# An operand made earlier, denser weight conversions and a shared mixing step in an attention and channel-mix kernel

## The chip, the cores and the metric

The kernel runs on one core of a Trainium2 chip. The metric is the device time in microseconds (us), the median of several runs. Beside the runs there is one profiled execution, from which the page and all answers of the trace come.

## The reference

```python
def _attn_ref(q, k, v):                      # q, k, v: 8 x 12 x 448 x 64
    scale = 1.0 / np.sqrt(q.shape[-1])
    scores = scale * np.matmul(q, k.transpose(0, 1, 3, 2)) - np.log(S)
    attn = 1.0 / (1.0 + np.exp(-scores))
    return np.matmul(attn, v).astype(np.float32)

def _moe_ref(x, mu_k, mu_r, w_k, w_v, w_r):  # x: 8 x 448 x 768, heads side by side
    x_prev = np.concatenate([np.zeros((B, 1, D)), x[:, :-1, :]], axis=1)
    xk = mu_k * x + (1.0 - mu_k) * x_prev
    xr = mu_r * x + (1.0 - mu_r) * x_prev
    k = np.maximum(xk @ w_k, 0.0)            # w_k: 768 x 1024
    v = k * k @ w_v                          # w_v: 1024 x 768
    r = 1.0 / (1.0 + np.exp(-(xr @ w_r)))    # w_r: 768 x 768, the "receptance"
    return (r * v).astype(np.float32)
```

The attention uses a sigmoid of each score and no sum over a row. Its output, with heads side by side, is the input of the channel mix. Inputs are scaled in `setup_inputs`. The weights arrive as 64-bit floats.

## The kernel before, in words

**Attention (lines 447 to 473).** 48 pairs of heads are taken two at a time, so 24 rounds ("pairs" from here on, since the code's index `n` steps by two), each of NV = 7 steps over blocks of 64 keys. In a step TensorE computes scores into `sc` (line 317), ScalarE turns them into probabilities `pf` (one sigmoid of 128 x 896 elements, line 320), and two steps later (`LAG`) TensorE multiplies them with the values into `av` (line 329). `sc` has two buffers in PSUM, `pf` has `PFB` = 4 in SBUF, `raw` (queries and keys) and `vn` (values) have six each, so their loads are issued two rounds before they are needed. `av` has four PSUM banks, two per round.

After the seventh step of a round `gather` (lines 336 to 346) mixes each finished head pair with its own copy shifted by one position. It does so twice, for `xr` and for `xk`: GpSimd sets the first column to zero, VectorE multiplies the shifted rows by 1 − mu (line 344), VectorE adds mu times the rows (line 345), and SP stores the result `xo` to HBM as `xr_d` or `xk_d`. `xo` has eight buffers.

**Conversions (lines 204 to 277).** VectorE turns each 64-bit weight into float32 by bit operations (lines 211 to 216), reading `wraw` (two buffers) and writing one of the seven `wbit` buffers; line 244 then forms sums and differences. Each call of `convert_next` does one block. During attention there are 24 blocks: twelve of `w_r`, whose results are split into two parts in the `slot` tiles (lines 289 and 290), and twelve of `w_k`, whose results are stored to HBM as `wk_o`. The 16 blocks of `w_v` come in the second plan and are stored as `wv_o`.

**Mixing half (lines 477 to 597).** Three stages: receptance (`xr` times `w_r`), key (`xk` times `w_k`), value (squared keys times `w_v`). Each goes over four pairs of token groups (`s` = 0 to 3; a group is one batch of 448 tokens). For such a pair a matrix product in two by two blocks is done with seven products instead of eight, in `ORDER` = (0, 1, 4, 5, 6, 2, 3). Every product needs one operand from the tokens: `right` fetches rows into a y buffer (`fetch`, line 394; SP), subtracts others where needed (`minus`, line 402; VectorE), and `operand` splits the result into a high part (a cast on ScalarE, line 408) and a remainder (VectorE, line 409). A matmul in float32r runs three times, high by high, high by remainder and remainder by high (line 524), into PSUM banks `xb` or `yb`. `evacuate` combines banks and writes results (lines 537 to 576), and `load_weight` brings the next stage's weights into the slots (lines 508 to 510) during the last pass of a stage.

The operand's home comes from `take`: a ring of four in stages 0 and 1, two in `rra` and two in `rrb`, and three larger ones in stage 2. The y buffers come from `y_of`: roles 0 and 1 in `ysa`, 2 and 3 in `ysb`. `rra` and `ysa` lie in a pool that exists from the start; `rrb` and `ysb` lie in the pool `kp`, opened where attention's buffers (`raw`, `vn`, `pf`, `xo`) lay, so each of its tiles has to wait for the old tiles at its place.

**The order of the work.** Both halves are planned by `Plan`: each operation has an engine, a modelled cost, a priority (the argument `at`) and dependencies, and a list scheduler picks on each engine the ready operation with the lowest priority number. Its result fixes the order on each engine; every engine then runs its queue in order. The two plans are emitted one after the other, each in a block of manual order; operations of the second may slip between those of the first on an engine. The planner does not know dependencies between reads of the same data.

Before the change the operands of products 0 and 1 of the first pair are planned in the attention half:

```python
    right(0, 0, 0, N - 6)
    right(0, 0, 1, N - 5)
```

and product 4, the third, is the first of the second plan that needs `ysb` and `rrb`.

Of the kernel before, what the change touches and what calls it, by code (L numbers as in the profile page):

```python
# [22 lines left out]
class Plan:  # L23
# [7 lines left out]
    def op(self, engine, cost, prio, run, reads, writes, dma=None):  # L31
        i = len(self.ops)
        deps = set()
        for r in reads:
            if r in self.writer:
                deps.add(self.writer[r])
        for w in writes:
            if w in self.writer:
                deps.add(self.writer[w])
            deps.update(self.readers.get(w, ()))  # L40
        for r in reads:
            self.readers.setdefault(r, []).append(i)
        for w in writes:
            self.writer[w] = i
            self.readers[w] = []
        deps.discard(i)
        self.ops.append(Op(engine, cost, prio, run, deps, dma))
# [51 lines left out]
def attention_then_channel_mix(  # L99
# [15 lines left out]
    nc = tc.nc  # L115
# [36 lines left out]
    wk_o = [dram.tile([P, WO], F32, name=f"wk_o{p}") for p in range(7)]  # L152
    wv_o = [dram.tile([P, WO], F32, name=f"wv_o{p}") for p in range(7)]

    WP, PFB, RAW, WB = 512, 4, 6, 7

    def ring(pool, name, bufs, shape, dtype):
        return [pool.tile(shape, dtype, name=f"{name}{i}") for i in range(bufs)]
# [3 lines left out]
    slots = [wp.tile([P, 2 * WO], F32R, name=f"slot{g}") for g in range(7)]  # L162
    RU = 2 * NJH
    wp.tile([P, 16], F32, name="gap0")
    rra = wp.tile([P, 2 * RU, TB], F32R, name="rra")
    ysa = wp.tile([P, RU, TB], F32, name="ysa")
    wraw = wp.tile([P, 2, WP, 2], U32, name="wraw")
    wbit = wp.tile([P, WB, WP], U32, name="wbit")
# [19 lines left out]
    def act(n, sbuf=False, ptr=False):  # L188
        return 51 + 0.834 * n + 42 * sbuf + 93 * ptr

    def dve(n, fast=False, ptr=False):
        return 69 + n / (1.92 if fast else 0.96) + 61 * ptr
# [143 lines left out]
    def gather(n, at):  # L336
        b, j = divmod(n, NP)
        x, X = av[bank(n)], ("av", bank(n))
        for mu, om, dst, key in ((mur, omr, xr_d, "xr_d"), (muk, omk, xk_d, "xk_d")):
            u = nxo[0] % len(xo)  # L340
            nxo[0] += 1
            y, Y = xo[u], ("xo", u)
            op(POOL, 200, at, lambda y=y: nc.gpsimd.memset(y[:, 0:1], 0.0), [], [Y])
            op(DVE, dve(S, ptr=True), at, lambda y=y, om=om: nc.vector.tensor_scalar_mul(y[:, 1:], x[:, :S - 1], om[:, j:j + 1]), [X, ("om", key)], [Y])  # L344
            op(DVE, dve(S, ptr=True), at, lambda y=y, mu=mu: nc.vector.scalar_tensor_tensor(y, x[:, :S], mu[:, j:j + 1], y, ALU.mult, ALU.add), [X, Y], [Y])  # L345
            dma(dst[b][:, j], y, at, [Y], [(key, n)])

# [5 lines left out]
    def units(name, u, n):  # L353
        return big[name][:, u:u + n], [("wraw", x % 2) if name == "wraw" else (name, x) for x in range(u, u + n)]

    def y_of(stage, role):
        if stage < 2:
            return units(("ysa", "ysb")[role // 2], role % 2 * NJH, NJH)
        return units(("wbit", "ysb", "ysa", "wraw")[role], 0, NFH)

    first_of_value = 2 * NS * 7

    def take(stage):
        u = rr_n[0]
        rr_n[0] += 1
        if stage < 2:
            name, at = ("rra", "rrb")[u % 4 // 2], u % 2 * RU
            return units(name, at, NJH), units(name, at + NJH, NJH)
        u -= first_of_value
        if u % 3 < 2:  # L370
            name = ("rra", "rrb")[u % 3]
            return units(name, 0, NFH), units(name, NFH, NFH)
        return units("rra", 2 * NFH, NFH), units("rrb", 2 * NFH, NFH)

    def pieces(g):
        lo, hi, found = g * TB, (g + 1) * TB, []
# [2 lines left out]
            found.append((b, slice(x0 - b * S, x1 - b * S), slice(x0 - lo, x1 - lo)))  # L379
        return found  # L380

    def fetch(stage, g, ch, role, at):
        y, Y = y_of(stage, role)
        n = TILES[stage]
        rows = slice(ch * n, (ch + 1) * n)
        if stage == 2:
            dma(y, k2_d[g][:, rows], at - 0.5, [("k2_d", g, f) for f in range(ch * n, (ch + 1) * n)], Y)
            return
        src, key = ((xr_d, "xr_d"), (xk_d, "xk_d"))[stage]
        parts = pieces(g)  # L390

        def go():
            for b, cs, cd in parts:
                nc.sync.dma_start(y[:, :, cd], src[b][:, rows, cs])

        reads = [(key, b * NP + j) for b, _, _ in parts for j in range(ch * n, (ch + 1) * n)]
        op(SP, 500 * len(parts), at - 0.5, go, reads, Y, dma=P * n * TB * 4 / 300)

    def minus(stage, dst, a, b, at):
        (d, D_), (x, X), (y, Y) = (y_of(stage, r) for r in (dst, a, b))  # L400
        for t in range(TILES[stage]):
            op(DVE, dve(TB), at, lambda t=t: nc.vector.tensor_sub(d[:, t], x[:, t], y[:, t]), [X[t], Y[t]], [D_[t]])  # L402

    def operand(stage, role, keys, at):
        y, Y = y_of(stage, role)
        (hi, H), (lo, L) = take(stage)
        for t in range(TILES[stage]):
            op(ACT, act(TB, True), at, lambda t=t: nc.scalar.copy(hi[:, t], y[:, t]), [Y[t]], [H[t]])  # L408
            op(DVE, dve(TB), at, lambda t=t: nc.vector.tensor_sub(lo[:, t], y[:, t], hi[:, t]), [Y[t], H[t]], [L[t]])  # L409
        for k in keys:  # L410
            used[k] = (hi, lo, H + L)

    def right(stage, s, p, at):
        g0, g1 = 2 * s, 2 * s + 1
        key = [(stage, s, p)]
        if p == 0:
            fetch(stage, g0, 0, 0, at)
            operand(stage, 0, key, at)
        elif p == 1:
            fetch(stage, g0, 1, 1, at)  # L420
            operand(stage, 1, key, at)
        elif p == 4:
            fetch(stage, g1, 0, 2, at)
            minus(stage, 0, 2, 0, at)
            operand(stage, 0, key, at)
        elif p == 5:
            fetch(stage, g1, 1, 3, at)
            minus(stage, 0, 3, 0, at)
            operand(stage, 0, key, at)
            minus(stage, 1, 1, 0, at)  # L430
        elif p == 6:
            minus(stage, 2, 3, 2, at)
            operand(stage, 2, key, at)
        elif p == 2:
            operand(stage, 3, key, at)
        else:
            operand(stage, 1, key, at)

    for n in range(4):
        load(n, -9 + n // 2 * 2)  # L440
# [6 lines left out]
    def convert_next(at, after):  # L447
        try:
            work.send((at, after))
        except StopIteration:  # L450
            pass
# [3 lines left out]
    for t in range(T + LAG):  # L455
        n, j = t // NV * 2, t % NV
        if t < T:
            if j == 0:
                convert_next(n + 8, n - 2 if n else None)
            score(n, j, t, n + j / NV)  # L460
        if t < LAG:
            continue
        n, j = (t - LAG) // NV * 2, (t - LAG) % NV
        weigh(n, j, t - LAG, n + j / NV)
        if j == NV - 1:
            for m in (n, n + 1):
                gather(m, m)
                if m + 4 < N:
                    load(m + 4, n + 0.5)
    right(0, 0, 0, N - 6)  # L470
    right(0, 0, 1, N - 5)
    with tc.manual_schedule():
        plan.emit()
    att.close()
    ps.close()

    kp = ctx.enter_context(tc.tile_pool(name="kp", bufs=1, side="right", reuse_waits="tile"))
    rrb = kp.tile([P, 2 * RU, TB], F32R, name="rrb")
    ysb = kp.tile([P, RU, TB], F32, name="ysb")
    big["rrb"], big["ysb"] = rrb, ysb  # L480
    p1s = ring(kp, "p1s", 4, [P, TB], F32)
# [30 lines left out]
    def multiply(stage, s, p, i, at):  # L512
        xs = p in (0, 1, 4, 2)
        bank, K = (xb[i], ("xb", i)) if xs else (yb[i], ("yb", i))
        first = p in (0, 5, 4)
        hi, lo, R = used[stage, s, p]
        whi, wlo, W = slot_of(stage, p)
        n, w = TILES[stage], WIDTH[stage]

        def go():  # L520
            for t in range(n):
                c = slice(t * w + i * P, t * w + (i + 1) * P)
                for e, (a, b) in enumerate(((whi[:, c], hi[:, t]), (whi[:, c], lo[:, t]), (wlo[:, c], hi[:, t]))):
                    nc.tensor.matmul(bank, a, b, start=first and t == 0 and e == 0, stop=t == n - 1 and e == 2, skip_group_check=True)  # L524

        reads = R + [W + (h, a) for h in range(WO // WC) for a in ("hi", "lo")]
        op(PE, mm(3 * n, TB), at, go, reads, [K])
# [50 lines left out]

    work = conversions(((2, w_v, put_dram(wv_o, WIDTH[2])),))
    next(work)  # L580
    for a in range(4 * TILES[2]):
        convert_next(2 + 2.5 * a, None)
    PREP, EVAC = -1.0, 0.3
    at = 0
    for stage in range(3):
        for s in range(NS):
            for p in ORDER:
                if (stage, s, p) not in used:
                    right(stage, s, p, at + PREP)
                for i in range(ROWS[stage]):  # L590
                    multiply(stage, s, p, i, at + i / ROWS[stage])
                    evacuate(stage, s, p, i, at + i / ROWS[stage] + EVAC)
                if stage < 2 and s == NS - 1:
                    load_weight(stage + 1, p, at + 1.2)
                at += 1
# [36 lines left out]
```

## Time and profile before

| what | value |
|---|---|
| median of 3 runs | 829.41 us (829.18 to 830.04) |
| profiled execution, its own time | 828.44 us |
| profiled execution, span from first to last instruction | 826.7 us |
| TensorE matmuls, busy | 811.3 us, 98% of the span |
| VectorE busy | 643.5 us, 78% |
| ScalarE busy | 444.7 us, 54% |
| DMA, mean rate over the span | 217 GB/s |
| mean granted TensorE clock | 0.995 |

The profiled execution's own time holds the span and 1.7 us around it. In the profile a row of a group names line, engine, operation, output and inputs by the program's tile names, the shapes and the count; behind the bar stand the busy time and the mean duration of one in ns; behind the second bar stands the engine's idle time just before these instructions and what ended most of it. PE is TensorE, DVE VectorE, ACT ScalarE, POOL GpSimd, SP SyncE, which issues all DMAs here. Rows of a timeline have the start, the duration up to the last one's end, and the count of merged instructions. Attention takes the span from 3.6 to 258.2 us, the mixing half the rest.

### The profile page before, as it was taken

Reading aid. Unit: us, or ns where it says so; the run is one execution under the profiler, and the core shown is the slowest. Engines: PE = TensorE matmul, PEld = TensorE weight load, DVE = VectorE, ACT = ScalarE, POOL = GpSimd, SP = SyncE. Lnnn points to the kernel's source line nnn. Section 1 sums busy time; section 2 is a strip of 40 time slices with the busy share of each in tenths; the row PEclk is TensorE's granted clock in tenths of the full one; section 3 lists DMA queues with packets and bytes.
Section 4 is the critical chain, followed back from the end, with each engine's and each line's share of the span. In section 5 each row is a group of like instructions: output and inputs, shape, how many; then the busy total and the mean of one; then the engine's idle time right before and its main releaser. Section 6 shows DMA issues by size and latency. Waiting matters only on the chain.

```text
span 826.7 us, 15158 instructions
## 1 busy us (share of the span) xinstructions
PE 811.3 (98%) x5460; PEld 638.0 (77%) x5460; DVE 643.5 (78%) x1200; ACT 444.7 (54%) x743; POOL 9.7 (1%) x100
## 2 busy tenths in 40 slices
PE   8999999999999699999999999999999999999997
PEld 3444444444446599999999999999999999999997
DVE  1988787878786799999999738466697794977955
ACT  5777666666663444546684746647694333333320
POOL 0000000000000000000000000000000000000000
PEclk9999999999999899999999999999999999999999
DMA  8897778898974777585969542422765546755414
GB/s 283 283 314 260 247 253 267 295 326 299 330 239 153 264 254 249 162 274 171 349 219 309 199 148 90 157 93 108 267 219 187 173 145 198 223 179 177 136 45 156
DMA packets 94203, 179.80 MB, mean 217 GB/s; under 512 B 10544, under 2 KB 74544, under 8 KB 94128
## 3 DMA queue, kind: packets, MB, share of 16 engines
q1 hardware_dynamic: 94128, 178.83, 64.9%
q8 instruction: 43, 0.70, 0.4%
q14 instruction: 32, 0.26, 0.1%
HBM read 109.06 MB, written 69.73 MB: 216 GB/s over the span
## 4 chain that ended last, share of the span: by engine, by line
PE 96%; DVE 2%; DMA 1%; issue 1%; ACT 0%; SPq 0%; DVEq 0%; ACTq 0%
PE xb L524 37%; PE yb L524 29%; PE sc L317 15%; PE av L329 15%; DMA ysb<-xr_d 1%; DVE xo L345 0%; DMA raw<-in_qk 0%; DVE xo L344 0%; DVE wbit L215 0%; DVE wbit L214 0%; DVE wbit L216 0%; DVE wbit L244 0%; DVE ysa L402 0%; DVE cc L576 0%; DVE cc L549 0%
## 5 line engine op out<-in xcount | busy, mean ns | idle before, releaser
L320 ACT ACTIVATE pf<-sc 128x896 f32<-128x896 f32 x168 | 154.0, 917 | 90.4 <-PE sc L317 90.2
L524 PE MATMUL xb<-rra,slot 128*128 128x448 f32 x828 | 180.7, 362 | 0.0
L524 PE MATMUL xb<-rrb,slot 128*128 128x448 f32 x756 | 167.4, 365 | 7.1 <-ACT cc L537 7.1
L317 PE MATMUL sc<-raw 64*64 64x448 f32 x1344 | 161.6, 541 | 3.6 <-DMA raw<-in_qk 3.6
L524 PEld LDWEIGHTS xb<-rra,slot 128*128 128x128 f32 x828 | 155.2, 188 | 10.9 <-issue 0.7
L329 PE MATMUL av<-pf,vn 64*64 64x448 f32 x1344 | 159.7, 536 | 0.0
L524 PEld LDWEIGHTS xb<-rrb,slot 128*128 128x128 f32 x756 | 142.8, 189 | 17.6 <-ACT cc L537 7.5
L524 PE MATMUL yb<-rra,slot 128*128 128x448 f32 x630 | 134.6, 362 | 0.0
L524 PEld LDWEIGHTS yb<-rra,slot 128*128 128x128 f32 x630 | 118.1, 188 | 7.8
L524 PE MATMUL yb<-rrb,slot 128*128 128x448 f32 x558 | 119.7, 362 | 0.0
L317 PEld LDWEIGHTS sc<-raw 64*64 64x64 f32 x1344 | 58.8, 134 | 72.4 <-issue 63.4
L329 PEld LDWEIGHTS av<-pf,vn 64*64 64x64 f32 x1344 | 58.4, 133 | 67.9 <-issue 66.8
L524 PEld LDWEIGHTS yb<-rrb,slot 128*128 128x128 f32 x558 | 104.7, 188 | 7.0
L408 ACT CAST rrb<-ysa 128x448 fp32r<-128x448 f32 x68 | 36.9, 562 | 39.6 <-DVE ysa L402 13.3
L344 DVE TENSOR_SCALAR xo<-av,omr 128x447 f32<-128x447 f32 x48 | 32.5, 677 | 31.9 <-PE av L329 31.6
L408 ACT CAST rra<-ysa 128x448 fp32r<-128x448 f32 x68 | 36.9, 561 | 27.1 <-PE xb L524 10.5
L562 DVE TENSOR_TENSOR u<-yb,p1s 128x448 f32<-128x448 f32 x40 | 24.9, 621 | 30.0 <-PE yb L524 29.8
L409 DVE TENSOR_TENSOR rra<-ysa,rra 128x448 fp32r<-128x448 f32 x64 | 37.5, 616 | 7.7 <-ACT rra L408 7.7
L560 ACT COPY p1s<-xb 128x448 f32<-128x448 f32 x40 | 21.1, 529 | 39.1 <-PE xb L524 39.0
L409 DVE TENSOR_TENSOR rrb<-ysa,rrb 128x448 fp32r<-128x448 f32 x68 | 39.6, 616 | 0.2 <-ACT rrb L408 0.2
L542 ACT ACTIVATE cc<-cc 128x448 f32<-128x448 f32 x48 | 27.5, 577 | 19.4 <-DVE cc L568 13.2
L408 ACT CAST rra<-ysb 128x448 fp32r<-128x448 f32 x44 | 23.9, 565 | 26.0 <-PE yb L524 14.3
(57 smaller groups left out, 744.2 us busy)
## 6 DMA issues: line engine op xcount, KB each, us to landing
k_d<-cc SPq DMA_DIRECT2D x64, 224.0 KB, 2.1
raw<-in_qk SPq DMA_DIRECT2D x48, 256.0 KB, 4.1
vn<-in_v SPq DMA_DIRECT2D x48, 224.0 KB, 5.2
xr_d<-xo SPq DMA_DIRECT2D x48, 224.0 KB, 3.8
xk_d<-xo SPq DMA_DIRECT2D x48, 224.0 KB, 3.8
r_d<-cc SPq DMA_DIRECT2D x48, 224.0 KB, 2.7
out<-cc SPq DMA_DIRECT2D x48, 224.0 KB, 3.0
raw<-in_qk SPq DMA_DIRECT2D x48, 192.0 KB, 4.2
```

The source lines that it names most:

```text
L317: nc.tensor.matmul(u[half[h ^ (m % 2)], m % 2, :S], x[half[h], c], x[half[h], D:D + S], start=True, stop=True)
L320: op(ACT, act(2 * S), at, lambda: nc.scalar.activation(f, u[:, :, :S], AF.Sigmoid, bias=NEG_LOG_S, scale=SCALE), [("sc", t % 2)], [("pf", ...
L329: nc.tensor.matmul(av[bank(m)][half[r ^ (m % 2)], :S], vn[m % RAW][half[r], j, :], pf[t % PFB][half[r], m % 2, :], start=j == 0, stop=j == ...
L344: op(DVE, dve(S, ptr=True), at, lambda y=y, om=om: nc.vector.tensor_scalar_mul(y[:, 1:], x[:, :S - 1], om[:, j:j + 1]), [X, ("om", key)], [Y])
L408: op(ACT, act(TB, True), at, lambda t=t: nc.scalar.copy(hi[:, t], y[:, t]), [Y[t]], [H[t]])
L409: op(DVE, dve(TB), at, lambda t=t: nc.vector.tensor_sub(lo[:, t], y[:, t], hi[:, t]), [Y[t], H[t]], [L[t]])
L524: nc.tensor.matmul(bank, a, b, start=first and t == 0 and e == 0, stop=t == n - 1 and e == 2, skip_group_check=True)
L542: op(ACT, act(TB), at, lambda: nc.scalar.activation(c, src, AF.Relu), R, [C])
L560: op(ACT, act(TB), at, lambda: nc.scalar.copy(p1s[i], x), [X], [P1])
L562: op(DVE, dve(TB), at, lambda: add(u2[i], y, p1s[i]), [Y, P1], [U2])
```

## The change

- The operand of product 4 of the first pair of receptance is made within the attention half, like those of products 0 and 1. For it `rra` grows from two to three places of operands and `rrb` shrinks from two to one, and `y_of` puts roles 2 and 3 of the very first pair into `wbit` instead of `ysb`. `PFB` goes from 4 to 3.
- `take` goes round the same four places (and three larger ones in the last stage), now counted through `rra` and on into `rrb`.
- The 24 conversions of the attention half are spread over 18 rounds instead of 24: in every third round two are called. Their priority is `n + 4` instead of `n + 8`.
- The 16 conversions of `w_v` begin at the eighth product of the mixing half and come at every second product, instead of at 2, 4.5, 7 and so on.
- In `gather` the multiplication of the shifted rows for `xk` is done by ScalarE (`nc.scalar.mul` with a per-partition factor); that for `xr` stays on VectorE, and so do both additions.

```diff
-    WP, PFB, RAW, WB = 512, 4, 6, 7
+    WP, PFB, RAW, WB = 512, 3, 6, 7
...
-    rra = wp.tile([P, 2 * RU, TB], F32R, name="rra")
+    rra = wp.tile([P, 3 * RU, TB], F32R, name="rra")
...
-            op(DVE, dve(S, ptr=True), at, lambda y=y, om=om: nc.vector.tensor_scalar_mul(y[:, 1:], x[:, :S - 1], om[:, j:j + 1]), [X, ("om", key)], [Y])
+            if key == "xr_d":
+                op(DVE, dve(S, ptr=True), at, lambda y=y, om=om: nc.vector.tensor_scalar_mul(y[:, 1:], x[:, :S - 1], om[:, j:j + 1]), [X, ("om", key)], [Y])
+            else:
+                op(ACT, act(S, ptr=True), at, lambda y=y, om=om: nc.scalar.mul(y[:, 1:], x[:, :S - 1], om[:, j:j + 1]), [X, ("om", key)], [Y])
...
-    def y_of(stage, role):
+    def y_of(stage, s, role):
+        if stage == s == 0 and role > 1:
+            return units("wbit", (role - 2) * NJH, NJH)
         if stage < 2:
             return units(("ysa", "ysb")[role // 2], role % 2 * NJH, NJH)
...
     def take(stage):
         u = rr_n[0]
         rr_n[0] += 1
+        n = TILES[stage]
         if stage < 2:
-            name, at = ("rra", "rrb")[u % 4 // 2], u % 2 * RU
-            return units(name, at, NJH), units(name, at + NJH, NJH)
-        u -= first_of_value
-        if u % 3 < 2:
-            name = ("rra", "rrb")[u % 3]
-            return units(name, 0, NFH), units(name, NFH, NFH)
-        return units("rra", 2 * NFH, NFH), units("rrb", 2 * NFH, NFH)
+            at = [u % 4 * RU + t for t in range(RU)]
+        else:
+            at = [(u - 2 * NS * 7) % 3 * 2 * n + t for t in range(2 * n)]
+        found = []
+        for x in at:
+            name, x = ("rra", x) if x < 3 * RU else ("rrb", x - 3 * RU)
+            found.append((big[name][:, x], (name, x)))
+        return tuple(zip(*found[:n])), tuple(zip(*found[n:]))
...
             if j == 0:
-                convert_next(n + 8, n - 2 if n else None)
+                for _ in range(1 + (n % 6 == 4)):
+                    convert_next(n + 4, n - 2 if n else None)
...
-    right(0, 0, 0, N - 6)
-    right(0, 0, 1, N - 5)
+    for p in ORDER[:3]:
+        right(0, 0, p, N - 6 + p)
...
-    rrb = kp.tile([P, 2 * RU, TB], F32R, name="rrb")
+    rrb = kp.tile([P, RU, TB], F32R, name="rrb")
...
-    for a in range(4 * TILES[2]):
-        convert_next(2 + 2.5 * a, None)
...
                 if (stage, s, p) not in used:
                     right(stage, s, p, at + PREP)
+                if at >= 7 and at % 2 == 0:
+                    convert_next(at + 1, None)
```

`fetch`, `minus`, `operand` and `right` take the pair's index `s` as a further argument and pass it to `y_of`, and the high and remainder parts of an operand are now tuples of single tiles (`hi[t]` in place of `hi[:, t]`).

More of the change, by code (lines that the diff above doesn't have):

```diff
@@ L359, in y_of @@
         return units(("wbit", "ysb", "ysa", "wraw")[role], 0, NFH)
-    first_of_value = 2 * NS * 7
     def take(stage):
@@ L380, in pieces, with fetch @@
         return found
-    def fetch(stage, g, ch, role, at):
-        y, Y = y_of(stage, role)
+    def fetch(stage, s, g, ch, role, at):
+        y, Y = y_of(stage, s, role)
         n = TILES[stage]
@@ L397, in fetch, with minus, operand @@
         op(SP, 500 * len(parts), at - 0.5, go, reads, Y, dma=P * n * TB * 4 / 300)
-    def minus(stage, dst, a, b, at):
-        (d, D_), (x, X), (y, Y) = (y_of(stage, r) for r in (dst, a, b))
+    def minus(stage, s, dst, a, b, at):
+        (d, D_), (x, X), (y, Y) = (y_of(stage, s, r) for r in (dst, a, b))
         for t in range(TILES[stage]):
             op(DVE, dve(TB), at, lambda t=t: nc.vector.tensor_sub(d[:, t], x[:, t], y[:, t]), [X[t], Y[t]], [D_[t]])
-    def operand(stage, role, keys, at):
-        y, Y = y_of(stage, role)
+    def operand(stage, s, role, keys, at):
+        y, Y = y_of(stage, s, role)
         (hi, H), (lo, L) = take(stage)
         for t in range(TILES[stage]):
-            op(ACT, act(TB, True), at, lambda t=t: nc.scalar.copy(hi[:, t], y[:, t]), [Y[t]], [H[t]])
-            op(DVE, dve(TB), at, lambda t=t: nc.vector.tensor_sub(lo[:, t], y[:, t], hi[:, t]), [Y[t], H[t]], [L[t]])
+            op(ACT, act(TB, True), at, lambda t=t: nc.scalar.copy(hi[t], y[:, t]), [Y[t]], [H[t]])
+            op(DVE, dve(TB), at, lambda t=t: nc.vector.tensor_sub(lo[t], y[:, t], hi[t]), [Y[t], H[t]], [L[t]])
         for k in keys:
-            used[k] = (hi, lo, H + L)
+            used[k] = (hi, lo, list(H + L))
     def right(stage, s, p, at):
@@ L416, in right @@
         if p == 0:
-            fetch(stage, g0, 0, 0, at)
-            operand(stage, 0, key, at)
+            fetch(stage, s, g0, 0, 0, at)
+            operand(stage, s, 0, key, at)
         elif p == 1:
-            fetch(stage, g0, 1, 1, at)
-            operand(stage, 1, key, at)
+            fetch(stage, s, g0, 1, 1, at)
+            operand(stage, s, 1, key, at)
         elif p == 4:
-            fetch(stage, g1, 0, 2, at)
-            minus(stage, 0, 2, 0, at)
-            operand(stage, 0, key, at)
+            fetch(stage, s, g1, 0, 2, at)
+            minus(stage, s, 0, 2, 0, at)
+            operand(stage, s, 0, key, at)
         elif p == 5:
[L427 to L430, printed above, removed]
+            fetch(stage, s, g1, 1, 3, at)
+            minus(stage, s, 0, 3, 0, at)
+            operand(stage, s, 0, key, at)
+            minus(stage, s, 1, 1, 0, at)
         elif p == 6:
-            minus(stage, 2, 3, 2, at)
-            operand(stage, 2, key, at)
+            minus(stage, s, 2, 3, 2, at)
+            operand(stage, s, 2, key, at)
         elif p == 2:
-            operand(stage, 3, key, at)
+            operand(stage, s, 3, key, at)
         else:
-            operand(stage, 1, key, at)
+            operand(stage, s, 1, key, at)
     for n in range(4):
@@ L522, in go @@
                 c = slice(t * w + i * P, t * w + (i + 1) * P)
-                for e, (a, b) in enumerate(((whi[:, c], hi[:, t]), (whi[:, c], lo[:, t]), (wlo[:, c], hi[:, t]))):
+                for e, (a, b) in enumerate(((whi[:, c], hi[t]), (whi[:, c], lo[t]), (wlo[:, c], hi[t]))):
                     nc.tensor.matmul(bank, a, b, start=first and t == 0 and e == 0, stop=t == n - 1 and e == 2, skip_group_check=True)
```

## The prediction

> **What bounds the kernel now.** I read the page's head and its matmul groups first, then TensorE's waits, then the chain around the one stall, then each engine's timeline there.
>
> ```profile
> PE 811.3 (98%) x5460; PEld 638.0 (77%) x5460; DVE 643.5 (78%) x1200; ACT 444.7 (54%) x743; POOL 9.7 (1%) x100
> L524 PE MATMUL xb<-rra,slot 128*128 128x448 f32 x828 | 180.7, 362 | 0.0
> L524 PE MATMUL xb<-rrb,slot 128*128 128x448 f32 x756 | 167.4, 365 | 7.1 <-ACT cc L537 7.1
> L524 PE MATMUL yb<-rra,slot 128*128 128x448 f32 x630 | 134.6, 362 | 0.0
> L524 PE MATMUL yb<-rrb,slot 128*128 128x448 f32 x558 | 119.7, 362 | 0.0
> ...
> PE xb L524 <- ACT cc L537: 7.1, 1, 7.1
> PE sc L317 <- DMA raw<-in_qk: 3.6, 1, 3.6
> ```
>
> TensorE is the bound at 98%, and it waits only twice: at the start for its first load, and once for 7.1 us in the mixing half. The chain shows where, the clock windows what it costs beyond that.
>
> ```profile
> 269.96 4.71 DMA ysb<-xr_d
> 274.69 0.64 DVE ysa L402
> 275.82 0.55 ACT cc L537
> 276.41 7.29 PE xb L524 x27
> 305.31 16.20 PE xb L524 x81
> 814.72 7.22 PE yb L524 x36
> ...
> 258.22 11.08 PE L524 MATMUL xb<-rra,slot 128*128 128x448 f32 x54
> 276.41 7.29 PE L524 MATMUL xb<-rrb,slot 128*128 128x448 f32 x27 [7.10 <-ACT cc L537]
> ...
> 272.50:276.40 3.90, 0.00 (x0) 0.00 (x0) 1.71 (x4) 1.05 (x3) 0.00 (x0) 0.55 0.97 384
> 276.40:279.70 3.30, 3.29 (x8) 2.78 (x9) 3.30 (x7) 2.45 (x6) 0.00 (x0) 0.50 1.06 397
> ```
>
> In steady state 81 matmuls take 16.20 us, 0.200 each. Products 0 and 1 (54 matmuls, 10.80 us) run from 258.22; the third, product 4, should follow at 269.02 and starts at 276.41: 7.39 us lost. Its 27 matmuls then take 7.29 instead of 5.40, 1.89 us more, and the granted clock says why: 0.50 until 279.7. Together 9.28. Check: the four groups hold 2772 matmuls, 554.4 us at 0.200, and the chain runs from 258.22 to 814.72 + 7.22 = 821.94, which is 563.72: 9.3 us over, so the rest of the mixing half has no stall. That is the pool to win.
>
> Why product 4 is late:
>
> ```profile
> 246.21 0.33 SPq L202 DMA_DIRECT2D wraw<-in_moe_w_v  x1
> 269.55 0.32 SPq L202 DMA_DIRECT2D xk_d<-xo  x1
> 269.96 0.90 SPq L394 DMA_DIRECT2D ysb<-xr_d  x2
> ...
> 254.32 0.36 DVE L212 TENSOR_SCALAR wbit<-wraw 128x384 uint32<-128x384 uint32 x1 [6.08 <-DMA wk_o<-wbit]
> 254.59 0.68 DVE L344 TENSOR_SCALAR xo<-av,omr 128x447 f32<-128x447 f32 x1
> 258.14 0.68 DVE L345 SCALAR_TENSOR_TENSOR xo<-av,mur,xo 128x448 f32<-128x448 f32 x1
> 258.73 0.68 DVE L345 SCALAR_TENSOR_TENSOR xo<-av,muk,xo 128x448 f32<-128x448 f32 x1
> 259.32 0.42 DVE L212 TENSOR_SCALAR wbit<-wraw 128x512 uint32<-128x512 uint32 x1
> 262.78 0.35 DVE L213 TENSOR_SCALAR wexpo<-wraw 128x384 uint32<-128x384 uint32 x1
> 268.84 0.68 DVE L345 SCALAR_TENSOR_TENSOR xo<-av,muk,xo 128x448 f32<-128x448 f32 x1
> ```
>
> Its fetch stands on SP behind the last mixed rows (269.55), and these are late on VectorE: a conversion sat 6.08 us waiting for a buffer's store, the gather of the last pair but one came after it, another conversion followed (259.32 to 262.78), and the last gather ended at 269.5, though attention ended at 258.2.
>
> **The change part by part.**
>
> *Third operand in attention.* One fetch, three subtractions, three casts and three remainders move from after 269.96 to inside attention; the fetch needs batch 1, stored early, and weight buffers that the earlier conversions leave free. On SP it is one issue of about 0.4 us, ahead of loads that stand two pairs (21 us) before their use. On VectorE six operations by the 0.53 us of the start-to-start steps (three take 1.70), 3.2 us, on ScalarE three casts: beside TensorE, whose steps cover them, so zero on the path; uncovered they would cost at most what they cost today, the 6.45 us from 269.96 to 276.41. After attention TensorE then has 3 × 5.40 = 16.2 us of products instead of 10.8, to 274.4. The fourth operand (product 5) is late next: its fetch now writes weight buffers, so it waits for nothing that attention's end releases, and SP issues such a thing early when it can (the `in_moe_w_v` load at 246.21 belongs to the second plan). Gain: 7.39, and with no idle time no half clock: 1.89.
>
> The Trainium skill (TensorE: Matmul & The Clock Gate, Part 1) says that the array's clock falls to half after an idle window of about 3.4 us and rises after as much activity; the trace agrees, with 0.50 to 0.55 after 272.5. By that rule an idle rest shorter than the window costs only itself.
>
> *Conversions in fewer cycles.* 24 conversions move from 24 pairs into 18 (four per three pairs). One costs VectorE 3.46 us (259.32 to 262.78); per pair of 10.5 us that adds 1.15, while the mixing gives 2 × 0.59 = 1.19 to ScalarE. VectorE stays at its mean, and for the last six pairs it has only the gather. So neither the 6.08 us wait nor the conversion at 259.32 stands before the last gather, which should end near 263, not 269.5. DMA is the other side:
>
> ```profile
> 214.40:224.90 10.50, 10.50 (x116) 4.87 (x112) 9.21 (x17) 6.40 (x8) 0.42 (x5) 1.00 1.00 351
> 4.00:256.50 252.50, 252.50 (x2672) 116.43 (x2672) 190.88 (x348) 163.45 (x195) 9.14 (x88) 1.00 0.83 280
> ...
> wraw<-in_moe_w_k SPq DMA_DIRECT2D x12, 512.0 KB, 6.4
> wk_o<-wbit SPq DMA_DIRECT2D x21, 256.0 KB, 4.5
> ```
>
> A third of a conversion more per pair in the second nine pairs is (512 + 21/12 × 256)/3 = 320 KB, some 31 GB/s. The busiest pair of now, the row with 351, ran at a full share without a PE stall; a backlog of a few us meets a lead of 21. I take zero; bounds 0 and the waits priced in the third rival.
>
> *Mixing on ScalarE.* 48 multiplications, two per pair, in front of the sigmoids in ScalarE's queue:
>
> ```profile
> L560 ACT COPY p1s<-xb 128x448 f32<-128x448 f32 x40 | 21.1, 529 | 39.1 <-PE xb L524 39.0
> ...
> DVE xo L344 <- PE av L329: 31.6, 16, 4.5
> DVE wbit L212 <- DMA wraw<-in_moe_w_k: 6.8, 4, 2.4
> DVE wbit L212 <- DMA wk_o<-wbit: 6.1, 1, 6.1
> ...
> 251.33 0.95 PE L329 MATMUL av<-pf,vn 64*64 64x448 f32 x8
> 252.08 0.95 PE L317 MATMUL sc<-raw 64*64 64x448 f32 x8
> 255.09 0.95 PE L317 MATMUL sc<-raw 64*64 64x448 f32 x8
> ...
> 253.14 0.92 ACT L320 ACTIVATE pf<-sc 128x896 f32<-128x896 f32 x1 [0.59 <-PE sc L317]
> ```
>
> The nearest row is the PSUM copy, 0.53. ScalarE idles 0.59 of each 1.50 us step, so two in a row push one sigmoid by some 0.5. A score computed at 252.08 has its sigmoid from 253.14 to 254.06, and its buffer is wanted at 255.09: about 1.0 us of slack, and the next steps regain 0.59 each. Bounds per pair: 0, and what exceeds 1.0. No row shows ScalarE and VectorE reading one `av` bank; if they take turns, the first waits for VectorE's (0.68 by L344 at 254.59). With a last `av` product ending at 252.28 (251.33 + 0.95), the sigmoid starts at 252.28 + 0.68 + 2 × 0.53 = 254.02 instead of 253.14, 0.9 us late: just inside the slack. I take 0.3 us over all pairs; ends 0 and 6 (0.25 in each of 24, when a cast stands in between).
>
> The Trainium skill (PSUM — Partial Sum Buffer, PSUM bank collisions raise a hardware error) says that two engines may not access one bank and quadrant at once, reads against reads included, so software must order them. That speaks for the turns and against this edit; no run here shows it yet. By ScalarE: Activation LUTs, What ACT_TABLE_LOAD costs, a per-partition scale adds about 93 ns: an estimate of 0.62 for one, which would push the sigmoid by 0.2 more.
>
> *Buffers, one edit each way.* Three probability buffers instead of four: a sigmoid of step t overwrites those of t−3, whose product was issued before score t, so nothing waits: zero. The operand ring keeps four places (three of `rra`, one of `rrb`) and three in the last stage: zero. *The last 16 conversions* begin at step 8, every two steps instead of 2.5, later than before until the fourteenth:
>
> ```profile
> 290.00:328.00 38.00, 38.00 (x192) 35.60 (x191) 37.97 (x78) 19.04 (x36) 0.00 (x0) 1.00 0.74 245
> ```
>
> VectorE is full there and TensorE is not delayed, because conversions yield to operands by priority. If that cover went, each would cost up to its 3.46 us; I take zero, since the load moves away from the first, tightest pass.
>
> Sum: −7.39 − 1.89 + 0.3 = −9.0 against the profiled execution's own 828.44 (span 826.7), thus 819.4; the median of the runs is 829.41, 0.97 above it, and gives 820.4.
>
> **The rivals.** *Attention pays for the turns.* The pushed sigmoids pass the slack in many pairs, for 1 to 6 us: 821 to 826, centre 823. For it: the margin of 0.1 us above. Against: only two such commands in 10.5 us, and regained time after each.
>
> *The fourth operand is late.* SP could still put its fetch behind the last mixed rows. From issue to first matmul it takes 6.45 us now; issued at 263 it would be there at 269.5, in time for 274.4, and issued as late as today it would cost 276.4 − 274.4 = 2.0: 820.4 + 2.0 = 822.4. Against: the 246.21 row.
>
> *Slower: VectorE's waits become TensorE's.* Today a VectorE stuck on a conversion's DMA delays only gathers. Now, where ScalarE's multiplication is ordered after VectorE's, a late VectorE holds ScalarE's queue, and with it the sigmoids and TensorE. All such waits of today reaching it (6.8 + 6.1 = 12.9, less five slacks of 0.1) cost 12.4: 829.4 − 9.3 + 12.4 = 832.5; it decides from 9.3 on. For it: the DMA share of 1.00. Against: VectorE waited for `av` itself in 16 of 24 pairs, and the 6.1 lay in the end that is now empty.
>
> *The change doesn't do what it says:* the weight buffers come free only at the end, the third operand stays late, and the time stays at 829.
>
> **How the numbers follow.** Forecast 0.64 (819.4 to 821.0), attention pays 0.18, fourth operand late 0.06, slower 0.07, no change 0.05. From 819.4 to 825 the first three leave out about 0.14. Faster by over 0.2% (1.7 us, about what a measurement of this kernel can tell from no change): 0.64 + 0.18 + 0.06 less a little, 0.87; same 0.05; slower 0.08.
>
> **What would show it.** Right: no wait between products 1 and 4, `rra` as operand of the first 81 matmuls, granted clock 1.00 throughout, the last gather done by 264, about 554.4 us from the first product to the last. Wrong: waits of `sc` L317 or `av` L329 for `pf` L320 in attention; a wait in product 5; VectorE waits for `av` that end late, with ScalarE behind them.

## The result, and the profile after

The changed kernel takes 824.68 us (824.11 to 824.86) against 829.43 before: a ratio of 0.9942, 95% interval 0.9929 to 0.9955, 4.75 us less. The forecast was 820.4, with 819.4 to 821.0 around it, so the gain came to about half of the 9.0 us that were summed up, and the time lies in the first rival's range of 821 to 826. The profiled execution has a span of 823.1 instead of 826.7.

The head of the page after, and TensorE's two rows of the mixing half's start (start, duration, engine, line, shapes, count). In the changed kernel lines 345 and 347 are the multiplications of VectorE and ScalarE in `gather`, 348 the additions, 289 and 290 the split of `w_r`, 399 the fetch and 530 the mixing half's matmul; in the experiments these numbers shift by a few.

```profile
PE 812.9 (99%) x5460; PEld 622.9 (76%) x5460; DVE 615.1 (75%) x1152; ACT 467.1 (57%) x791; POOL 10.3 (1%) x100
...
263.66 16.48 PE L530 MATMUL xb<-rra,slot 128*128 128x448 f32 x81
279.98 5.56 PE L530 MATMUL yb<-rrb,slot 128*128 128x448 f32 x27
```

The 81 matmuls of the first three products now run as one group without a wait, and the fourth product follows. In the chain the last product ends at 818.36, so from the first product to there it is 554.7 us where 554.4 were computed and 563.7 were used before: 9.0 of the 9.3 us are gone, the half clock with them. But the first product starts at 263.66 instead of 258.22. Attention became 5.44 us longer, and 9.0 − 5.44 is the 3.6 us by which the spans differ.

Where attention lost it, from the waits of the kernel after (who waited for whom: us in total, times, longest):

```profile
PE sc L317 <- DMA raw<-in_qk: 3.5, 1, 3.5
PE sc L317 <- ACT pf L320: 1.7, 5, 0.6
...
ACT xo L347 <- DVE xo L345: 9.3, 16, 2.0
ACT slot L289 <- DVE wbit L216: 5.4, 6, 1.4
...
DVE xo L345 <- ACT xo L347: 25.2, 21, 1.9
```

The two engines wait for each other in the mixing: ScalarE 9.3 us for VectorE's multiplication at the same `av` bank, VectorE 25.2 us for ScalarE's at the next one. TensorE's waits for a sigmoid are listed as 1.7 us only, since the modelled end of a matmul lies beyond the start of the next and hides part of each; the matmul counts in windows of one round show the rest (a full round has 116):

```profile
35.60:46.10 10.50, 9.81 (x104) 3.52 (x100) 10.28 (x22) 8.63 (x14) 0.60 (x4) 1.00 0.86 299
56.60:67.10 10.50, 9.98 (x108) 3.87 (x104) 8.26 (x17) 8.92 (x14) 0.39 (x4) 1.00 0.90 316
```

By the starts of TensorE's groups of eight matmuls, 0.752 us apart when nothing is late, there are nine stalls of 0.2 to 0.8 us after the start, most with one or two of 0.05 behind it, 4.3 us together; eight of them lie before 111 us, where the casts of `w_r` also pass through ScalarE. Four of the nine, 2.4 us, follow multiplications of ScalarE that had to wait for a late VectorE. Five, 1.3 us, follow casts of `w_r`: in four of them a cast had waited 0.9 to 1.4 us for its weights from VectorE, in the fifth ScalarE's multiplications come behind two casts. The other 1.1 us lies at the very start:

```profile
7.00:9.50 2.50, 2.50 (x30) 1.23 (x32) 0.00 (x0) 1.73 (x2) 0.00 (x0) 1.00 0.98 336
7.00:9.50 2.50, 2.50 (x18) 1.05 (x18) 0.00 (x0) 0.97 (x2) 0.00 (x0) 1.00 1.05 387
```

The first row is of before, the second of after. The first scores run at half rate, in this profile of before until about 7 us, in this one of after until about 9: 12 matmuls at 0.09 us. Nine of the experiments' profiles show 18 to 32 in the same window with the same work, so this differs between executions. It would account for the spans of the two profiles differing by 3.6 where the medians differ by 4.75; the executions without a profile do not show it. The 1.00 in these two rows is no measurement of the whole window: the trace's first record of the granted clock begins at 6.6 us before and at 9.2 us after, just where the slow start ends, and a stretch without a record is printed as full clock.

One of the stalls, from the timeline of the kernel after (rows of other work left out, here and below):

```profile
62.76 0.93 PE L317 MATMUL sc<-raw 64*64 64x448 f32 x8
63.74 0.68 DVE L345 TENSOR_SCALAR xo<-av,omr 128x447 f32<-128x447 f32 x1
64.45 1.16 ACT L347 ACTIVATE xo<-av,omk 128x447 f32<-128x447 f32 x2 [0.54 <-DVE xo L345]
65.49 1.72 ACT L320 ACTIVATE pf<-sc 128x896 f32<-128x896 f32 x2
65.64 0.68 DVE L345 TENSOR_SCALAR xo<-av,omr 128x447 f32<-128x447 f32 x1 [1.22 <-ACT xo L347]
66.46 0.98 PE L317 MATMUL sc<-raw 64*64 64x448 f32 x8 [0.52 <-ACT pf L320]
```

VectorE, just done with a remainder, takes its multiplication at 63.74. ScalarE's two stand in its queue and may not read that bank before 64.42; they take 1.16 together. Only at 65.49 does the sigmoid run for the scores issued at 62.76, and TensorE, which wants that score buffer back, loses 0.70 us by its starts (0.52 in the list, by the modelled end). VectorE's second multiplication then waits 1.22 for ScalarE's, so all that follows on VectorE is late as well, the weights that ScalarE is to cast among it.

### The profile page after: what moved, and what is told of

The parts are those of the page before. It is cut to its first block, busy times and chain, and to the rows that moved or that the text cites. A ratio compares the mean times of both kernels' runs of the same rounds, so it can differ in the third digit from the quotient of the medians.

```text
span 823.1 us, 15181 instructions
## 1 busy us (share of the span) xinstructions
PE 812.9 (99%) x5460; PEld 622.9 (76%) x5460; DVE 615.1 (75%) x1152; ACT 467.1 (57%) x791; POOL 10.3 (1%) x100
## 4 chain that ended last, share of the span: by engine, by line
PE 90%; DVE 4%; ACT 2%; DMA 2%; issue 1%; SPq 0%; ACTq 0%; DVEq 0%
PE xb L530 39%; PE yb L530 29%; PE sc L317 12%; PE av L329 11%; DVE xo L348 1%; ACT pf L320 1%; DMA raw<-in_qk 1%; ACT xo L347 1%; DMA wraw<-in_moe_w_r 1%; DVE wbit L216 0%; DVE wbit L215 0%; DVE wbit L214 0%; DVE xo L345 0%; DMA wk_o<-wbit 0%; DVE wbit L244 0%
## 5 line engine op out<-in xcount | busy, mean ns | idle before, releaser
L530 PE MATMUL xb<-rra,slot 128*128 128x448 f32 x1188 | 249.8, 362 | 0.0
L530 PEld LDWEIGHTS xb<-rra,slot 128*128 128x128 f32 x1188 | 222.7, 188 | 15.5 <-issue 0.7
L530 PE MATMUL yb<-rra,slot 128*128 128x448 f32 x927 | 193.0, 362 | 0.0
L530 PEld LDWEIGHTS yb<-rra,slot 128*128 128x128 f32 x927 | 173.8, 187 | 11.6
L530 PE MATMUL xb<-rrb,slot 128*128 128x448 f32 x396 | 89.1, 362 | 0.0
L345 DVE TENSOR_SCALAR xo<-av,omr 128x447 f32<-128x447 f32 x48 | 32.5, 681 | 73.6 <-PE av L329 47.1
L530 PEld LDWEIGHTS xb<-rrb,slot 128*128 128x128 f32 x396 | 74.2, 187 | 5.0
L530 PE MATMUL yb<-rrb,slot 128*128 128x448 f32 x261 | 57.5, 362 | 0.0
L530 PEld LDWEIGHTS yb<-rrb,slot 128*128 128x128 f32 x261 | 48.9, 187 | 3.3
L413 ACT CAST rra<-wbit 128x448 fp32r<-128x448 f32 x46 | 24.4, 566 | 29.7 <-PE yb L530 29.1
L414 DVE TENSOR_TENSOR rra<-ysb,rra 128x448 fp32r<-128x448 f32 x54 | 31.4, 617 | 13.0 <-ACT rra L413 13.0
```

What stands on the lines that cost most here:

```text
L413: op(ACT, act(TB, True), at, lambda t=t: nc.scalar.copy(hi[t], y[:, t]), [Y[t]], [H[t]])
L414: op(DVE, dve(TB), at, lambda t=t: nc.vector.tensor_sub(lo[t], y[:, t], hi[t]), [Y[t], H[t]], [L[t]])
```

## The experiments

Theory 1: the turns at the `av` banks make ScalarE, VectorE and with them the sigmoids late. Theory 2: the denser conversions crowd the engines. Theory 3: three probability buffers are too few.

**Mixing back on VectorE.**

```diff
-            if key == "xr_d":
-                op(DVE, ... nc.vector.tensor_scalar_mul(...))
-            else:
-                op(ACT, ... nc.scalar.mul(...))
+            op(DVE, ... nc.vector.tensor_scalar_mul(...))
```

> The changed kernel with both multiplications of the mixing on VectorE again, all else kept. Theory 1 (the turns of ScalarE and VectorE at one av bank make both late, and the sigmoids with them): attention loses almost nothing, the first product starts near 258.2 us, the time is about 820.4 (819.8 to 821.5), and ScalarE has no wait for L289 casts worth naming. Theory 2 (the denser conversions crowd both engines): most of the loss stays, 823 to 825, with the sigmoids behind casts. Theory 3 (three probability buffers instead of four): no change, 824.7.

Measured 820.66 (819.70 to 820.88), ratio 0.9896 (0.9882 to 0.9909). Without this one part the change gives 8.3 us instead of 4.75. Sigmoids are gone from TensorE's list of waits, and the first product starts 4.1 us earlier than in the changed kernel, 0.3 of it from a shorter slow start:

```profile
PE sc L317 <- DMA raw<-in_qk: 3.8, 2, 3.5
...
259.53 16.48 PE L527 MATMUL xb<-rra,slot 128*128 128x448 f32 x81
```

One stall of 0.6 us was left in attention, behind two casts of an operand, and the conversions are as dense as in the changed kernel: theory 2 fell.

**ScalarE first at each bank.** The list of the two mixings is turned round, so that `xk` is planned ahead of `xr`, and the plan knows the turn (the lines on VectorE are those for `xr`, those on ScalarE for `xk`):

```diff
-  op(DVE, ..., [X, ("om", key)], [Y])
+  op(DVE, ..., [X, ("om", key), ("turn", bank(n))], [Y])
-  op(ACT, ..., [X, ("om", key)], [Y])
+  op(ACT, ..., [X, ("om", key)], [Y, ("turn", bank(n))])
```

> The changed kernel, but in the plan VectorE's multiplication at a bank comes after ScalarE's at the same bank, so ScalarE never stands behind VectorE there and the planner counts the turn. The work is the same. Theory 1: ScalarE's waits for VectorE's multiplication (9.3 us in the profile of the changed kernel) go to zero, the sigmoids are pushed by two multiplications only, about 0.5 us within 1.0 of slack, and the time is 820.4 to 821.5. Theory 2: 823 to 825, since casts and conversions are as dense as before. Theory 3: 824.7.

Measured 820.73 (819.83 to 821.03), ratio 0.9897 (0.9884 to 0.9911). Same instructions, same engines, another order: the loss is gone but for 0.3 us. ScalarE's row of waits for VectorE's multiplication is missing; VectorE waits instead, where it costs nothing:

```profile
ACT xo L347 <- PE av L329: 1.2, 1, 1.2
...
DVE xo L348 <- ACT xo L347: 46.5, 16, 6.7
```

**Different head pairs for the two engines.**

```diff
-            if key == "xr_d":
+            if n % 2:
```

> The changed kernel, but ScalarE does both multiplications of the even head pairs and VectorE both of the odd ones, so that the first commands of the two engines go to different av banks. The same count of multiplications on each engine. Theory 1: no first wait of ScalarE for VectorE, the time is 820.4 to 821.5, as with ScalarE first. Theory 2: 823 to 825. Theory 3: 824.7.

Measured 820.36 (819.59 to 821.71), ratio 0.9897 (0.9882 to 0.9912). ScalarE has no wait for VectorE's multiplication here either, and 0.5 us is lost in attention after the start. The three intervals overlap; which of these versions is best was not settled.

**Four probability buffers.**

```diff
-    WP, PFB, RAW, WB = 512, 3, 6, 7
+    WP, PFB, RAW, WB = 512, 4, 6, 7
...
-    xo = ring(apool, "xo", 8, [P, S], F32)
+    xo = ring(apool, "xo", 6, [P, S], F32)
```

> The changed kernel with four probability buffers again, paid for by six instead of eight buffers of mixed rows. Theory 1: the sigmoid's slack is set by the two score buffers, not by these, so the stalls stay: 824.7 (824 to 825.5). Theory 3: attention's stalls go and the time falls to about 820.5.

Measured 823.82 (823.58 to 824.78), ratio 0.9940 (0.9927 to 0.9952), which overlaps almost wholly with the changed kernel's interval; the time lies just under the expected 824 to 825.5. Eight of the nine stalls stand at the same places, most with the same sizes, 0.80 near 44 us and 0.70 near 65.5, and together they cost 4.1 us instead of 4.3: theory 3 fell.

**ScalarE's multiplication alone**, the one edit in the kernel before.

> The kernel before with one edit: the multiplication for xk on ScalarE. Theory 1: the turns alone cost TensorE in attention. The casts of w_r are fewer per round here, so less than the 4.3 us counted in the changed kernel: 2 to 4 us later at the first product, the stall before the third product stays near 9, time 831 to 834. Theory 2 (the loss needs the denser conversions): no stalls in attention, 829.4 or a little less as VectorE has less to do: 828.5 to 829.6.

Measured 833.76 (833.02 to 834.60), ratio 1.0056 (1.0043 to 1.0068): by itself this part makes the kernel slower, as theory 1 wanted. The expected range was met by luck, though: 2 to 4 us had been expected in attention and 9 at the third product, and the profile has 9.8 in attention after the start and 3.4 in the mixing half. Nine stalls of 0.2 to 0.5 us are spread over attention, and one large one stands near its end. The timeline of that one is the prediction's third rival, step by step:

```profile
257.83 0.36 DVE L212 TENSOR_SCALAR wbit<-wraw 128x384 uint32<-128x384 uint32 x1 [5.65 <-DMA wk_o<-wbit]
258.11 0.68 DVE L345 TENSOR_SCALAR xo<-av,omr 128x447 f32<-128x447 f32 x1
258.82 1.16 ACT L347 ACTIVATE xo<-av,omk 128x447 f32<-128x447 f32 x2 [4.96 <-DVE xo L345]
259.87 1.72 ACT L320 ACTIVATE pf<-sc 128x896 f32<-128x896 f32 x2
260.84 1.67 PE L317 MATMUL sc<-raw 64*64 64x448 f32 x8 [4.26 <-ACT pf L320]
...
265.59 0.93 PE L317 MATMUL sc<-raw 64*64 64x448 f32 x8
```

VectorE's wait for a weight store, harmless in the kernel before, reaches TensorE as 4.26 us. The granted clock is then 0.50 from 261.0 to 264.4, as the duration of 1.67 instead of 0.93 shows, and with it the place costs 6.2 us by TensorE's starts. In the changed kernel the conversions are over by then, so this one does not come.

**The same, ScalarE first.** The edit of the second experiment in the kernel before.

> The kernel before with the multiplication for xk on ScalarE, as in the run that had it alone (833.8 us), but with ScalarE first at each bank in the plan. Theory 1: a VectorE that is late (it waits some 6 us for a weight store near 250 us) no longer holds ScalarE, and attention loses under 1 us; the stall before the third product is as in the kernel before, so 828.5 to 830.5. If it is ScalarE's added work and not the order that delays the sigmoids: 832 to 834.

Measured 825.62 (824.67 to 827.38), ratio 0.9953 (0.9939 to 0.9967). In attention 0.2 us were lost after the start, so the order and not the added work delays the sigmoids. The stall after attention did not stay as it was, and the number was missed by 3 us on the good side:

```profile
253.54 0.36 DVE L212 TENSOR_SCALAR wbit<-wraw 128x384 uint32<-128x384 uint32 x1 [2.58 <-DMA wk_o<-wbit]
...
265.55 0.69 DVE L348 SCALAR_TENSOR_TENSOR xo<-av,mur,xo 128x448 f32<-128x448 f32 x1
...
275.00 7.63 PE L527 MATMUL xb<-rrb,slot 128*128 128x448 f32 x27 [4.25 <-ACT cc L540]
```

VectorE waited 2.58 for the store instead of 6.08 and finished its last gather at 266.2 instead of 269.5, and the wait before the third product was 4.25 instead of 7.10.

**All four multiplications of a round on ScalarE** (`if False:` in place of the test of `key`).

> The changed kernel with all four multiplications of a round on ScalarE. VectorE's additions then come second at every bank, so ScalarE waits for nobody there, but four commands of about 0.55 us stand before one sigmoid. By the slack of 1.0 us read from the trace the sigmoid is 2.2 less 0.6 = 1.6 us late and TensorE loses 0.6 us in each of 24 rounds, 14 us: 832 to 836, near 834.5. If only the order matters and ScalarE's load doesn't: 820.5.

Measured 833.40 (832.42 to 834.54), ratio 1.0044 (1.0030 to 1.0059). There is no turn to wait for here, only length, and the slack shows:

```profile
PE sc L317 <- ACT pf L320: 6.9, 23, 1.1
...
L347 ACT ACTIVATE xo<-av,omk 128x447 f32<-128x447 f32 x48 | 30.9, 644 | 0.0
...
272.23 16.47 PE L530 MATMUL xb<-rra,slot 128*128 128x448 f32 x81
```

23 waits, one in nearly every round, 12.4 us together by TensorE's starts where some 14 were expected. The first product comes 14.0 us later than in the kernel before; the rest is a longer slow start. Two multiplications fit in front of a sigmoid, four do not.

**The denser conversions alone**, in the kernel before.

```diff
-                convert_next(n + 8, n - 2 if n else None)
+                for _ in range(1 + (n % 6 == 4)):
+                    convert_next(n + 4, n - 2 if n else None)
```

> The kernel before with one edit: the 24 conversions in 18 rounds. If the stall before the third product comes from VectorE being behind with conversions when attention ends, the last gather ends some 5 us earlier (at about 264 instead of 269.5), the fetch goes out then and lands with its first cast 6.45 us later at 270.5, 1.5 us after the second product, too short an idle time for the clock to fall: the time falls by about 7 to 8 us to 821 to 823 with no third operand made early. Theory 1: no stalls in attention. Theory 2: stalls in attention of 3 to 4 us, so 824 to 826.

Measured 822.94 (822.29 to 823.46), ratio 0.9926 (0.9914 to 0.9939). No operand is made earlier here, and yet most of the stall goes, because VectorE is done with the gathers sooner:

```profile
262.57 0.68 DVE L345 SCALAR_TENSOR_TENSOR xo<-av,muk,xo 128x448 f32<-128x448 f32 x1
...
258.51 11.08 PE L525 MATMUL xb<-rra,slot 128*128 128x448 f32 x54
270.32 6.05 PE L525 MATMUL xb<-rrb,slot 128*128 128x448 f32 x27 [0.73 <-ACT cc L538]
```

The last gather ends at 263.3, and the third product comes 1.0 us after the second one's 10.80 instead of 7.4, its 27 matmuls at 6.05 instead of 7.29. The granted clock stays at 1.00. Attention has no stall after the start, against theory 2.

**The third operand alone**, mixing on VectorE and conversions at the old pace.

> The changed kernel with two parts undone: the mixing is on VectorE and the 24 conversions come one per round as before. Left are the third operand in attention, its buffers, and the later start of the last 16 conversions. Its y buffers are weight buffers that the last conversions still hold at the end of attention, so the fetch for the third operand goes out only after 262. If the early operand needs the denser conversions, the stall stays: 825 to 829.5. If the operand alone suffices, 820.4.

Measured 821.69 (821.04 to 821.77), ratio 0.9908 (0.9893 to 0.9923): neither of the two expected numbers, but near the second; the expected wait for the buffers until 262 did not come.

```profile
253.33 0.38 SPq L396 DMA_DIRECT2D wbit<-xr_d  x1
260.01 0.37 SPq L396 DMA_DIRECT2D wbit<-xr_d  x1
...
259.45 16.48 PE L526 MATMUL xb<-rra,slot 128*128 128x448 f32 x81
287.29 5.92 PE L526 MATMUL xb<-rra,slot 128*128 128x448 f32 x27 [0.56 <-DVE cc L570]
```

A weight buffer was free for the third operand's fetch at 253, not after 262; the three products run through, and a late VectorE costs 0.56 later on. So the two parts are two ways to the same stall: alone they give 6.2 and 7.4 us, together 8.3.

**Matmuls while TensorE waits for its first load**, on top of the split by head pairs.

```diff
+    op(DVE, 500, -30, lambda: nc.vector.memset(xo[7], 0.0), [], [("xo", 7)])
+    def heat():
+        for _ in range(3):
+            for m in range(2):
+                for h in range(2):
+                    nc.tensor.matmul(sc[0][half[h ^ m], m, :S], xo[7][half[h], :D], xo[7][half[h], :S], start=True, stop=True)
+    pe(heat, [("xo", 7)], [("sc", 0)], -30)
```

> The version with ScalarE and VectorE on different head pairs, and twelve matmuls on a zeroed buffer (their result is overwritten) in the 3.5 us in which TensorE waits for its first load. In the profiles the first scores take 0.65 us for what later takes 0.33, until 7 to 9 us into the span. If earlier activity ends the slow start earlier, 0.5 to 1.5 us are gained: 819 to 820. If the slow start has to do with the data's arrival, 820.4.

Measured 820.04 (819.75 to 820.87), ratio 0.9886 (0.9872 to 0.9900), not to be told from 820.36. The added matmuls ran from 1.41 to 5.6 us, past the first load's arrival at 3.5, and what they sped up they had taken. Their profile's slow start did end early, at 5.3 us by the first record of the granted clock, against 6.6 to 9.6 in the other eleven profiles, but it is one profile. What ends the slow start stays open.

## Why the prediction was right or wrong

- *The stall of 9.28 us* was right in size and went as a whole: 554.7 us from the first product to the end of the last. The granted clock has no dip left in the page's forty slices.
- *The fourth operand* was right: its fetch went out early, in attention. Below, the first fetch is the third operand's, the second the fourth's, and the third line is the last gather.

```profile
222.14 0.38 SPq L399 DMA_DIRECT2D wbit<-xr_d  x1
226.28 0.38 SPq L399 DMA_DIRECT2D wbit<-xr_d  x1
...
268.05 0.68 DVE L348 SCALAR_TENSOR_TENSOR xo<-av,muk,xo 128x448 f32<-128x448 f32 x1
```

- *The last gather* ends 5.0 us after attention (268.7 after 263.66). Near 263 had been said for attention's end at 258.2, which is the same distance.
- *Three buffers, the operand ring, the later conversions and the DMA rate*, each taken as zero, cost TensorE nothing that shows: it waits nowhere after 263.66, and after its first load it is the sigmoids, not loads, that it waits for in attention.
- *The third operand as the cause of the gain* was too narrow. The prediction named VectorE's backlog as the reason for the stall and still booked the whole gain on the operand; the denser conversions alone bring 6.2 of it.
- *Mixing on ScalarE* was the step that failed: 0.3 us over all rounds, where the trace has 4.3 and the two medians, each against its own kernel before, 3.6 (8.3 less 4.75). The mechanism was written down, as the first rival with 1 to 6 us and a centre of 823, and was given 0.18; the sign named for it, waits of `sc` for `pf`, is in the list of waits above. Three things in the term were off. One multiplication takes 0.63 us, not the 0.53 of the copy without a factor (the row below), which ate the margin of 0.1. VectorE was taken to start its first multiplication when the last `av` product ends, as in 22 of the 24 rounds before the change; now it starts 0.4 to 1.9 us later in nine of the 24 rounds. In four of these ScalarE's multiplication stands behind it, and a stall follows each time; in the other five ScalarE comes first, and a stall follows once, behind two casts. And the turn was charged to ScalarE only: VectorE's 25.2 us of waits, which the planner does not know, make the converted weights late, and ScalarE's casts wait for those (5.4 us) in front of the sigmoids.

```profile
L347 ACT ACTIVATE xo<-av,omk 128x447 f32<-128x447 f32 x48 | 27.8, 630 | 10.3 <-DVE xo L345 9.3 <-DMA raw<-in_qk 0.9
```

The Trainium skill (ScalarE: Activation LUTs, What ACT_TABLE_LOAD costs) adds about 93 ns for a per-partition scale, an estimate of 0.62 with the copy's 0.53, and 0.63 was measured. The Trainium skill (PSUM — Partial Sum Buffer, PSUM bank collisions raise a hardware error) asks for an order between two engines at one bank and quadrant, reads included; the waits between L345 and L347 agree with such an order, and they vanish where the two engines' multiplications go to different banks.

- *The slower rival* did not come in the changed kernel, and is real: with ScalarE's part alone TensorE waited 4.26 us in one place.

## What to carry to other kernels

An edit that shares a step between engines is priced by whom its new commands stand behind and what is queued behind them, not by their own length: 30 us of work moved to an engine 54% busy cost some 4 us of the bound one, and the same work with the other engine first cost nothing that could be measured. Before two engines read one PSUM bank, decide who goes first, give the engine that feeds TensorE the first turn or a bank of its own, and let the planner know of it. And where a stall has a backlog behind it, price clearing the backlog by itself; here it brought most of what the larger rebuild did.

## What the runs showed of the hardware

A VectorE wait of 5.65 us for a store reached TensorE as 4.26 us through ScalarE, though none of the three shares data there but one PSUM bank that two of them read. And the first scores run at half rate for 3 to 6 us after their start, by a length that differs between profiles of the same work (18 to 32 matmuls in the window from 7.0 to 9.5 us); it moves a single span by about 1 us. In every profile the first record of the granted clock begins only where this slow start ends (at 6.6 us in the one before, at 9.2 in the one after), so a clock of 1.00 printed ahead of it says nothing of the clock.
